# Half-size products for two more token blocks, paired masks, and V rows copied on the chip in a windowed attention plus squared-relu layer on one core

## The chip, the cores and the metric

The kernel runs on one core of a Trainium2 chip. The metric is device microseconds (us) of one execution; three runs of the kernel before took 288.63, 288.63 and 288.92 us, median 288.63. A profiled execution of the same kernel gives the trace that all readings below come from. Five engines work beside each other: TensorE (PE in the profile, with its weight loads as PEld), VectorE (DVE), ScalarE (ACT), GpSimd (POOL) and SyncE (SP). Here POOL does nearly nothing but issue loads, SP issues transposes and some loads and stores, and ACT issues stores beside its own work.

## The reference

Eight batches of 8 heads, 576 positions, 64 elements a head, all float32. Attention looks 32 positions to each side. Its output, 4608 tokens of 512 features, goes through a two-layer network whose hidden values (2048) are relu'd and squared.

```python
scores = q @ k.T / sqrt(64)                  # per batch and head
scores = where(abs(pos_q - pos_k) <= 32, scores, -1e9)
attn   = softmax(scores)
x      = (attn @ v) as [4608 tokens, 512]    # heads side by side
h      = x @ w_in                            # 512 -> 2048
out    = (relu(h) ** 2) @ w_out              # 2048 -> 512, float32
```

The kernel computes in bf16 with float32 sums in PSUM.

## The kernel before, in words

**Attention** goes in 24 steps (G in the code; three steps of 192 query positions for each batch, g = G % 3). The keys a step needs form two blocks of 128 positions (w = 0 and 1), starting at 192 g - 32 and 128 later. For each step:

- `load_qk` (L365) and `load_v` (L389) have POOL load q, k and v rows, casting to bf16 on the way. Step 0's k and step 2's q come as float32 through SP's and ACT's queues (`load_hw`, L374) and are cast on DVE and ACT. V goes into one of five tiles, `[128 positions, 2 key blocks, 8 heads, 66]`, a column of ones beside each head's 64. The second block of a step ends where the first block of the next step's first 64 rows do: block 1 of step g covers positions 192 g + 96 to 192 g + 224, and block 0 of step g + 1 begins at 192 g + 160. These 64 rows are loaded twice.
- q and k are turned by TensorE (`turn_pe`, L418, steps 0 to 8) or by a transposing DMA from SP (`turn_dma`, L449).
- `scores` (L468): 8 products for each key block (L495) into two PSUM banks, ACT takes the exponential into tile e (L518, 128x1024), DVE multiplies by a 0/1 mask into tile pt (L526, 128x1024). Each key block has a mask operation of its own.
- `pv` (L531): 8 products for each key block (L554) with V's ones giving the softmax sums, a reciprocal (L568), a scaled copy into xa or xb (L572), and a zeroing of half a PSUM region (L578 on ACT or L579 on DVE).
- `xturn` (L583) turns the result into `xt`, a ring of 1536 token columns.

**The first layer** takes tokens in blocks: 192, 192, 192, 192, 256, then 512 each (from token 1024). `mm1` (L637) is the standard form: for a 512-token block, 16 slices of hidden rows with 4 products of 512 columns each (L653), a relu for each slice out of PSUM (L629 on ACT or L628 on DVE) and a square for each two (L624 on DVE, L623 on ACT) into `gt`, a ring of 1024 tokens. `mm1s` (L696) is the half-size form, used for the blocks listed in `MM1S` (2560, 3072, 3584, 4096): 7 products of half-size matrices in place of 8. Four differences of x (L705) and, at the start of the kernel, sums of w_in (`sums_w1`, L684) are its operands; for each of 4 groups of hidden rows it runs 28 products of 256 columns (L733), a seed copy between two PSUM banks (L772), two copies out of PSUM (L634), two additions (L757), an in-place relu (L763 or L764), and relus and squares into `gt`.

**The second layer** is half-size for all but the first 512 tokens: `strassen` (L889) with products on L880, sums on L848, additions on L903, and stores. The first 512 tokens use `mm2` (L787, products on L798).

**What sets the order.** `record` (L929) lists all operations with their tiles; `rec` (L86) notes who reads and writes what. The string `ORDER` (L1039) gives each recorded operation, in that sequence, a letter for its engine (P TensorE, A ScalarE, D VectorE, G POOL, S SyncE) and a number; `apply` (L129) sorts by the number, and that sorted order is the order on every engine. Some operations can run on ACT or DVE (their `alt`), and the letter chooses. After the operations, ORDER gives each tile's slot in its pool (PSUM banks, e, pt, rt, oe, ...); a slot marked `w` is washed before use by one more product over zeros (L858). `fill` (L156) pads TensorE with small products over zeros (L295) until real work is dense. `emit` (L175) derives semaphore waits from the recorded reads and writes. No run-time choice is made: when an operation waits, everything behind it on its engine waits.

The dummy exponential of `setup_act` (L297), which makes ACT load its function table, has a place in ORDER like any other operation.

Of the kernel before, what the change touches and what calls it, by code (L numbers as in the profile page):

```python
# [4 lines left out]
ACTF = mybir.ActivationFunctionType  # L5
# [16 lines left out]
    MM1S=(2560, 3072, 3584, 4096),  # L22
# [9 lines left out]
    PAIR=(),  # L32
# [5 lines left out]
    SQP=1,  # L38
    FP=1,
    MP=0,  # L40
    S34=1,
    NZ=0,
    NV=5,
    NRAW=4,
    NE=2,
    NPT=3,
# [178 lines left out]
def dve(n, fast=True):  # L225
    return 153 + (0.52 if fast else 1.04) * n


class Gen:
# [130 lines left out]
    def source(self, t, b, g):  # L360
        t0, n = self.piece(t, b, g)
        src = (self.q if t == "q" else self.k)[b]
        return src[:, t0:t0 + n, :].rearrange("h (j p) d -> p j h d", j=2), n // 2

    def load_qk(self, t, b, g, key, after=None):  # L365
        s, h = self.source(t, b, g)
        G = 3 * b + g
        for j in range(2):
            dst = self.raw(t, b, g, j).rearrange("p (h d) -> p h d", h=8)
            self.p.rec("POOL", lambda e, j=j, dst=dst: e.dma_start(dst, s[:, j]),  # L370
                       writes=[self.rtag(t, b, g, j)], dma=(f"{t}{G % self.cfg['NRAW']}{j}", G), key=key, dur=500 + 3 * h,
                       move=(h // 2, 13.5), name=f"{t}{b}{g}{j}", after=after, slack=self.cfg["LSLACK"] if b > 1 else 0)

    def load_hw(self, t, g, eng, cast, u0, key):  # L374

        s, h = self.source(t, 0, g)
        for j in range(2):
# [4 lines left out]
            self.p.rec(eng, lambda e, j=j, f=f: e.dma_start(f.rearrange("p (h d) -> p h d", h=8), s[:, j]),  # L382
                       writes=[tag], dma=(f"h{t}{g}{j}", g), key=key, dur=450, move=(h // 2, 16), name=f"h{t}{g}{j}")
            fn = (lambda e, f=f, raw=raw: e.activation(raw, f, ACTF.Copy)) if cast == "ACT" else \
                (lambda e, f=f, raw=raw: e.tensor_copy(raw, f))
            self.p.rec(cast, fn, reads=[tag], writes=[self.rtag(t, 0, g, j)], key=self.cfg.get("CKEY", -100.0 - 14 + 100) + 3 * g,
                       dur=620 if cast == "ACT" else 600, name=f"c{t}{g}{j}")
# [13 lines left out]
    def load_w1(self, d, key):  # L401
        src = self.w_in[:, 512 * d:512 * d + 512].rearrange("(f p) c -> p f c", p=128)
        self.p.rec("POOL", lambda e: e.dma_start(self.W1[:, :, 512 * d:512 * d + 512], src),
                   writes=[("w1", d)], dma=(f"w1{d}", 0), key=key, dur=780, move=(32, 82), name=f"w1{d}")
# [13 lines left out]
    def turn_pe(self, t, b, g, key):  # L418
# [4 lines left out]
        v = Virt("bank", where=self.cfg.get("TB"))  # L423

        def f(e):
            ps = self.bank(v).bitcast(BF16)
            for j in range(4):
                for x in range(2):
                    mm = e.transpose(ps[:, n * j + h * x:n * j + h * x + h], raw[x][:, 128 * j:128 * j + 128],  # L429
                                     self.ID[0:h, 0:h])  # L430
            return mm
# [5 lines left out]
        def src():  # L437
            return self.bank(v).bitcast(BF16)[:, 0:4 * n].rearrange("p (j q) -> p j q", j=4)

        fa = lambda e: e.activation(dst, src(), ACTF.Copy)  # L440
        fd = lambda e: e.tensor_copy(dst, src())
        if t == "q":
            self.p.rec("ACT", fa, reads=[v], writes=w, key=key, dur=act(4 * n), name=f"ev{t}{b}{g}",
                       alt=("DVE", dve(4 * n), fd) if self.cfg["ALT"] else None, bias=0)
        else:
            self.p.rec("DVE", fd, reads=[v], writes=w, key=key, dur=dve(4 * n), name=f"ev{t}{b}{g}",
# [84 lines left out]
    def pv(self, G):  # L531
# [10 lines left out]
        for w in range(2):  # L542
# [15 lines left out]
            rd = [("v", G % NV, w), ("vset", G % NV), pt]  # L558
# [78 lines left out]
    def mm1(self, t0, n, ds, key, pair=False):  # L637
# [7 lines left out]
        v = Virt("bank", nb, clean=c >= 512, where=self.cfg.get("MB"))  # L645
        for h in range(nb):
# [10 lines left out]
            self.p.rec("PE", f, reads=[("xt", s) for s in steps] + [("w1", d // 4) for d in dh[:1]], writes=[(v, h)], uses=[v], key=key + 0.25 * h,  # L657
# [26 lines left out]
    def sums_w1(self, key):  # L684
        w, s, p = self.W1, self.SW, self.p
        for c in range(2):
            lo, hi = slice(512 * c, 512 * c + 512), slice(1024 + 512 * c, 1536 + 512 * c)
            a11, a12, a21, a22 = w[:, 0:2, lo], w[:, 2:4, lo], w[:, 0:2, hi], w[:, 2:4, hi]
            r1, r2 = [("w1", c)], [("w1", 2 + c)]
# [6 lines left out]
    def mm1s(self, t0, key):  # L696
# [11 lines left out]
        for m in range(4):  # L708
# [5 lines left out]
            wl, wh = [("w1", m // 2)], [("w1", 2 + m // 2)]  # L714
# [92 lines left out]
    def store(self, u, oe, dst, src, key, move):  # L807
# [3 lines left out]
                       move=move, name=f"st{u}", alt=("SP", 450, lambda e: e.dma_start(dst, src())), bias=self.cfg["STB"], after=self.stores[n - 8] if n >= 8 else None)  # L811
# [77 lines left out]
    def strassen(self, g, key):  # L889
# [5 lines left out]

        def out(i, j, rd, add, src, k, name):
            u = 4 * g + 2 * i + j
            oe = Virt("oe")
            o = lambda: self.oe(oe)
            if add is None:  # L900
# [139 lines left out]
D900 G1350 A1350 D1800 D8113 D8713 D9423 D10498 D8513 D10898 D12154 D7993 D7873 D9623 D10198 D7488 D7588 D21300 D10608  # L1040
D9908 D7198 D10298 D11118 D12354 D8313 D8933 D9223 D21953 D21015 D22183 D44470 D22063 D29378 S1350 D6598 S900 D4366
G1700 G2488 G4064 G5640 G4852 G3276 G7956 G7216 A900 A5559 A1780 A9625 G6428 G8696 G9580 G10464 G11348 G12128 G14572
G12908 G20264 G16140 G13688 G15352 G21044 G22564 P7268 A7873 P8259 A8811 P9715 A10350 D11468 P10140 A12274 D14614
P12224 D13658 D13928 A14839 P15537 D16007 D16277 P16505 P17033 A17473 P11390 D12554 P10907 A11459 P13176 A13811 D15299
# [132 lines left out]
```

## Time and profile before

| | |
|---|---|
| three runs, us | 288.63, 288.63, 288.92 |
| profiled execution, us | 288.32 |
| its span (first to last instruction), us | 286.5 |
| instructions | 7547 |
| bytes moved by DMA | 38.60 MB in 171106 packets |
| half-size first-layer products (L733) | 448 |
| standard first-layer products (L653) | 512, of them 192 with 512 columns |
| second-layer products (L880, L798) | 896 and 64 |

How to read the views: in a group's row stand line, engine, operation, the tile written and the tiles read, shape and count; then total busy us and mean ns of one; then how long the engine stood idle just before them, and what ended that wait. In a table of stretches each row is one stretch of time from the span's start, with busy us and counts for each engine, then the granted TensorE clock (1.00 is full), a DMA share and GB/s. The chain of work that ended last follows the execution backwards from its last instruction, each step to what released it. Matmul records of one group overlap each other in the trace, so counts and the pace of a back-to-back piece say more about TensorE than its busy share.

### The profile page before, as it was taken

To read this page: it belongs to the slowest core of one execution; us is meant where nothing else is said; L and a number is where in the kernel's file an instruction comes from. 1 tells how busy PE (TensorE), PEld (TensorE's weight loads), DVE (VectorE), ACT (ScalarE), POOL (GpSimd) and SP (SyncE) were. 2 spreads that over 40 slices of the span, in tenths; PEclk is the share of its full clock that TensorE was granted. 3 is DMA by queue.
4 is the path that set the end of the run, shared out by engine and by line. 5 is a ranking of instruction groups with operands and counts; after the bars stand their busy time and mean duration, and the time that the engine had idled before them with its cause. 6 is when DMAs were issued, how large, how long until landed. Compare 5 with 4: busy or idle time off the path is not lost.

```text
span 286.5 us, 7547 instructions
## 1 busy us (share of the span) xinstructions
PE 281.2 (98%) x3063; PEld 225.6 (79%) x3063; DVE 228.2 (80%) x427; ACT 200.3 (70%) x301; POOL 117.4 (41%) x153
## 2 busy tenths in 40 slices
PE   7999999999999999999999999999999999999995
PEld 7889857788657775667566888888988888888884
DVE  1878978868978798686998989988898978697731
ACT  2875738869783965777787978895688966778420
POOL 8999526999831927694332846000000000000000
PEclk9999999999999999999999999999999999999999
DMA  9999999999999999999999999995201221401033
GB/s 147 158 206 193 188 176 156 155 149 147 177 154 226 134 154 185 159 164 155 134 192 213 174 166 146 173 174 140 55 3 39 55 57 38 149 0 39 11 135 113
DMA packets 171106, 38.60 MB, mean 135 GB/s; under 512 B 158272, under 2 KB 170560, under 8 KB 171072
## 3 DMA queue, kind: packets, MB, share of 16 engines
q0 software_dynamic: 121920, 18.98, 99.4%
q1 hardware_dynamic: 42656, 13.51, 26.3%
q10 hardware_dynamic: 6496, 5.64, 7.2%
q8 instruction: 24, 0.39, 0.6%
q14 instruction: 10, 0.08, 0.2%
HBM read 38.80 MB, written 9.44 MB: 168 GB/s over the span
## 4 chain that ended last, share of the span: by engine, by line
PE 94%; DMA 2%; ACT 2%; DVE 1%; issue 0%; SPq 0%; DVEq 0%; ACTq 0%
PE ps L880 34%; PE ps L653 25%; PE ps L733 17%; PE ps L798 5%; PE ps L495 5%; PE ps L554 4%; DMA ts<-in_k_dram 2%; PE ps L429 2%; PE ps L295 1%; ACT kq L440 1%; PE ps L600 1%; PE ps L594 1%; DVE rt L757 0%; DVE rt L763 0%; ACT e L518 0%; DVE xa L572 0%
## 5 line engine op out<-in xcount | busy, mean ns | idle before, releaser
L653 PE MATMUL ps<-xt,w 128*128 128x192 bf16 (+2 forms) x512 | 77.4, 299 | 0.0
L629 ACT ACTIVATE rt<-ps 128x512 bf16<-128x512 f32 (+1 forms) x93 | 51.6, 566 | 30.1 <-PE ps L653 18.9
L653 PEld LDWEIGHTS ps<-xt,w 128*128 128x128 bf16 x512 | 44.6, 98 | 19.8
L396 POOL DMA_DIRECT2D v<-in_v_dram x48 | 41.9, 882 | 31.2 <-PE ps L554 31.2
L518 ACT ACTIVATE e<-ps 128x1024 bf16<-128x1024 f32 x48 | 48.1, 1021 | 8.3 <-PE ps L495 6.4
L880 PE MATMUL ps<-w,gt 128*128 128x256 bf16 x384 | 47.2, 273 | 0.0
L634 ACT ACTIVATE oe<-ps 128x512 f32<-128x512 f32 x56 | 32.6, 595 | 20.4 <-PE ps L880 10.9
L370 POOL DMA_DIRECT2D raw<-in_k_dram x46 | 36.8, 809 | 22.2 <-DMA kq<-raw 11.4
L623 ACT ACTIVATE gt<-rt 128x1024 bf16<-128x1024 bf16 (+2 forms) x49 | 41.6, 859 | 2.7 <-DVE rt L628 1.7
L880 PEld LDWEIGHTS ps<-w,gt 128*128 128x128 bf16 x384 | 36.7, 98 | 5.5
L526 DVE TENSOR_TENSOR pt<-e,mask 128x1024 bf16<-128x1024 bf16 x48 | 32.5, 685 | 8.5 <-ACT e L518 8.2
L370 POOL DMA_DIRECT2D raw<-in_q_dram x46 | 37.0, 812 | 5.2 <-DMA kq<-raw 2.9
L880 PE MATMUL ps<-ts,ss 128*128 128x256 bf16 x256 | 31.7, 273 | 0.0
L880 PE MATMUL ps<-ts,gt 128*128 128x256 bf16 x256 | 31.6, 273 | 0.0
L880 PEld LDWEIGHTS ps<-ts,ss 128*128 128x128 bf16 x256 | 24.7, 98 | 4.2
L880 PEld LDWEIGHTS ps<-ts,gt 128*128 128x128 bf16 x256 | 24.7, 98 | 3.5
L733 PE MATMUL ps<-xs,sw 128*128 128x256 bf16 x192 | 25.5, 273 | 0.0
L624 DVE TENSOR_TENSOR gt<-rt 128x1024 bf16<-128x1024 bf16 (+2 forms) x43 | 24.4, 576 | 1.3 <-ACT rt L629 1.1
L757 DVE TENSOR_TENSOR rt<-ps,oe 128x512 bf16<-128x512 f32 x32 | 21.6, 684 | 4.2 <-PE ps L733 3.8
L554 PEld LDWEIGHTS ps<-v,pt 128*128 128x128 bf16 x384 | 17.4, 98 | 3.9 <-DVE ps L579 0.8
L733 PEld LDWEIGHTS ps<-xs,sw 128*128 128x128 bf16 x192 | 18.5, 98 | 2.2
L554 PE MATMUL ps<-v,pt 128*128 128x65 bf16 x384 | 19.8, 194 | 0.1
(70 smaller groups left out, 370.2 us busy)
## 6 DMA issues: line engine op xcount, KB each, us to landing
out_dram<-oe ACTq DMA_DIRECT2D x20, 256.0 KB, 4.1
v<-in_v_dram POOLq DMA_DIRECT2D x32, 128.0 KB, 6.7
out_dram<-oe SPq DMA_DIRECT2D x16, 256.0 KB, 3.2
w<-in_moe_w_in_dram POOLq DMA_DIRECT2D x4, 512.0 KB, 9.6
w<-in_moe_w_out_dram POOLq DMA_DIRECT2D x4, 512.0 KB, 16.8
raw<-in_q_dram POOLq DMA_DIRECT2D x18, 96.0 KB, 6.2
raw<-in_q_dram POOLq DMA_DIRECT2D x14, 112.0 KB, 6.1
raw<-in_k_dram POOLq DMA_DIRECT2D x14, 112.0 KB, 6.5
```

Of the source, the lines that this page charges most:

```text
L370: self.p.rec("POOL", lambda e, j=j, dst=dst: e.dma_start(dst, s[:, j]), writes=[self.rtag(t, b, g, j)], dma=(f"{t}{G % self.cfg['NRAW']}{j ...
L396: self.p.rec("POOL", lambda e, j=j, lo=lo, hi=hi, k0=k0: e.dma_start(vt[lo - k0:hi - k0, j, :, 0:64], self.v[b, :, lo:hi, :].rearrange("h ...
L518: last = self.p.rec("ACT", lambda e, ef=ef, v=v: e.activation(ef(), self.bank(v, 0, 2), ACTF.Exp, scale=0.125), reads=[v], writes=tags, ke ...
L526: self.p.rec("DVE", lambda e, pf=pf, ef=ef, mb=mb, n=n: e.tensor_tensor(pf(y=0, n=n), ef(y=0, n=n).rearrange("p (w h q) -> p w h q", w=n, ...
L554: mm = e.matmul(ps[z:z + n, c:c + 65], ptt[:, 4 * (h % 2) + h // 2, z:z + n], vt[:, w, h, 0:65], start=((w == 0 or (z == 64 and split)) an ...
L623: alt = ("ACT", act(c), lambda e: e.activation(dst, src(), ACTF.Square)) if self.cfg["ALT"] else None
L624: self.p.rec("DVE", lambda e: e.tensor_tensor(dst, src(), src(), ALU.mult), reads=rd, writes=wr, key=key, dur=dve(c), name=name, alt=alt, ...
L629: return self.p.rec("ACT", lambda e: e.activation(dst(), src(), ACTF.Relu), reads=rd, writes=wr, key=key, dur=act(c), name=name, alt=alt, ...
L634: self.p.rec("ACT", lambda e: e.activation(dst(), src(), ACTF.Copy), reads=rd, writes=wr, key=key, dur=act(c), name=name, alt=alt, bias=se ...
L653: mm = e.matmul(ht[:, n * x:n * x + n], self.W1[:, ft, 128 * d:128 * d + 128], self.XT[:, ft, r:r + n], start=(ft == 0 and x == 0), stop=( ...
L733: mm = e.matmul(bk[:, 256 * x:256 * x + 256], lhs(k, 256 * m + 128 * x), rhs[:, k, :], start=start and x == 0 and k == 0, stop=(k == 1), s ...
L880: mm = e.matmul(op[:, 256 * y:256 * y + 256], lhs[:, l0[0] + k, a:a + 128], rhs[:, r0 + k, c0:c0 + 256], start=start and y == 0 and k == 0 ...
```

## The change

Three things are changed, and the whole order is written anew. The core of the diff:

```diff
 CFG = dict(
-    MM1S=(2560, 3072, 3584, 4096),
+    MM1S=(1536, 2048, 2560, 3072, 3584, 4096),
...
-    PAIR=(),
+    PAIR=(1024,),
...
-    MP=0,
+    MP=1,
...
+    VC=0,
...
-    NPT=3,
+    NPT=4,
...
+    def vcopy(self, G):
+        return G % 3 > 0 and G >= self.cfg["VC"]

     def load_v(self, b, g, key, after=None):
         G, NV = 3 * b + g, self.cfg["NV"]
         vt = self.V[G % NV]
         for j in range(2):
             k0 = 192 * g - 32 + 128 * j
             lo, hi = max(k0, 0), min(k0 + 128, S_)
+            if self.vcopy(G) and j == 0:
+                lo += 64
+                vs, vf = self.V[(G - 1) % NV][64:128, 1, :, 0:64], vt[0:64, 0, :, 0:64]
+                self.p.rec("DVE", lambda e, vs=vs, vf=vf: e.tensor_copy(vf, vs), reads=[("v", (G - 1) % NV, 1)], writes=[("vc", G % NV)],
+                           key=key + 2, dur=290, name=f"vc{b}{g}",
+                           alt=("ACT", act(512), lambda e, vs=vs, vf=vf: e.activation(vf, vs, ACTF.Copy)) if self.cfg["ALT"] else None,
+                           bias=self.cfg["ALTB"])
...
     def pv(self, G):
...
-            rd = [("v", G % NV, w), ("vset", G % NV), pt]
+            rd = [("v", G % NV, w), ("vset", G % NV), pt] + ([("vc", G % NV)] if w == 0 and cfg["VC"] < NG else [])
...
     def mm1(self, t0, n, ds, key, pair=False):
...
-            self.p.rec("PE", f, reads=[("xt", s) for s in steps] + [("w1", d // 4) for d in dh[:1]], writes=[(v, h)], uses=[v], key=key + 0.25 * h,
+            got = self.p.rec("PE", f, after=got, reads=[("xt", s) for s in steps] + [("w1", d // 4, d % 4 // 2 if d // 4 in self.cfg["W1H"] else 0) for d in dh[:1]], writes=[(v, h)], uses=[v], key=key + 0.25 * h,
                        dur=4 * len(dh) * (n / 2.4 + 2.5), name=f"A{t0}.{dh[0]}")
...
 ORDER = """
-D900 G1350 A1350 D1800 D8113 D8713 D9423 D10498 D8513 D10898 D12154 D7993 D7873 D9623 D10198 D7488 D7588 D21300 D10608
+D900 G1350 A48064 D5616 D7398 D7888 D8308 D9513 D8108 D9623 D11270 D4966 D5086 D1385 D9413 D2000 D9843 D10680 D5326
...
```

- **Half-size products:** the blocks at tokens 1536 and 2048 go from `mm1` to `mm1s`. The block at 1024 stays standard, with `PAIR`: two slices of hidden rows share two PSUM banks, one relu of 1024 and one square of 1024.
- **Masks:** with `MP=1`, steps 6 to 23 (those whose two key blocks are recorded together) take both slots of e and two neighbouring slots of pt, and one DVE operation of 128x2048 masks both key blocks after the second exponential. Steps 0 to 5 keep one mask operation for each block. The pool pt has 4 slots, not 3.
- **V rows:** in steps with g = 1 or 2 the first 64 rows of key block 0 are copied from the step before's tile (partitions 64 to 127 of block 1 to partitions 0 to 63 of block 0), on DVE or ACT, and the load takes the other rows only. PV of block 0 waits for the copy as well.
- **Order:** 1480 operations in place of 1418: on TensorE 466 in place of 442, DVE 447 for 427, ACT 339 for 322 (with stores that it issues), POOL 149 for 149, SP 79 for 78. Three slots are marked for a wash, where one was. In ORDER's first line the third entry is the dummy exponential: it stands at A1350 before and at A48064 after, behind ACT's casts of step 2's q.
- **Unused:** the diff also adds options (a split w_in load, another packing of q and k rows, a split last store) whose settings leave them off.

More of the change, by code (lines that the diff above doesn't have):

```diff
@@ L38 @@
     SQP=1,
+    W1H=(),
+    TAIL=0,
     FP=1,
-    MP=0,
+    MP=1,
     S34=1,
     NZ=0,
+    VC=0,
+    PR=0,
     NV=5,
@@ L894, in strassen @@
         u2, p5 = Virt("oe"), Virt("oe")
+        last = self.cfg["TAIL"] and g == NTOK // 512 - 1
         def out(i, j, rd, add, src, k, name):
@@ L899, in out @@
             o = lambda: self.oe(oe)
+            if last and add is None and i:
+                for y in range(2):
+                    c = slice(256 * y, 256 * y + 256)
+                    self.copy(lambda c=c: o()[:, c], lambda c=c: src()[:, c], rd, [(oe, y)], k, name + "ab"[y], 256, uses=[v, oe])
+                    dst = self.out[512 * g + 256 * i + 128 * y:512 * g + 256 * i + 128 * y + 128, 256 * j:256 * j + 256]
+                    self.store(f"{u}{'ab'[y]}", (oe, y), dst, lambda c=c: o()[:, c], k, (8, 21), uses=[oe])
+                return
             if add is None:
```

269 lines of the change are left out of this document (149 added, 120 removed), and 9 rows, old and new, of the table ORDER.

## The prediction

> **What bounds the kernel now.** I read the page's totals first, then the chain that ended last, then tables by stage, because an average over this kernel mixes attention, first layer and second layer.
>
> ```profile
> span 286.5 us, 7547 instructions
> ...
> PE 281.2 (98%) x3063; PEld 225.6 (79%) x3063; DVE 228.2 (80%) x427; ACT 200.3 (70%) x301; POOL 117.4 (41%) x153
> ...
> DMA  9999999999999999999999999995201221401033
> ...
> PE 94%; DMA 2%; ACT 2%; DVE 1%; issue 0%; SPq 0%; DVEq 0%; ACTq 0%
> ```
>
> TensorE carries 94% of the chain and looks busy for 98%. Ends of matmuls are modelled, so I check that figure with paces, from pieces of the chain in which products run back to back:
>
> ```profile
> 151.69 3.45 PE ps L653 x16
> 155.14 0.51 PE ps L554 x16
> ...
> 174.68 0.69 DVE rt L757
> ...
> 177.22 0.70 DVE rt L757
> ...
> 190.23 0.55 PE ps L495 x16
> ...
> 246.50 9.17 PE ps L733 x84
> ```
>
> A product of 512 columns (L653, first layer as it stands) takes 3.45/16 = 0.2156 us, one of 256 columns (L733, half-size) 9.17/84 = 0.1092, a PV product 0.51/16 = 0.0319, a score product 0.55/16 = 0.0344. Now the stage that the change rewrites, 100 to 170 us, counted by line on TensorE, without the weight loads:
>
> ```profile
> L653 PE MATMUL ps<-xt,w 128*128 128x512 bf16 x132 | 31.3, 379 | 0.0
> L880 PE MATMUL ps<-w,gt 128*128 128x256 bf16 x112 | 13.9, 273 | 0.0
> L880 PE MATMUL ps<-ts,gt 128*128 128x256 bf16 x86 | 10.7, 273 | 0.0
> L880 PE MATMUL ps<-ts,ss 128*128 128x256 bf16 x64 | 8.0, 273 | 0.0
> L554 PE MATMUL ps<-v,pt 128*128 128x65 bf16 x136 | 6.9, 194 | 0.0
> L495 PE MATMUL ps<-kq 64*128 64x128 bf16 x144 | 5.6, 217 | 0.0
> L733 PE MATMUL ps<-xt,w 128*128 128x256 bf16 x22 | 2.9, 272 | 0.0
> L733 PE MATMUL ps<-xs,sw 128*128 128x256 bf16 x4 | 0.6, 272 | 0.0
> ```
>
> 132 x 0.2156 + (262 + 26) x 0.1092 + 136 x 0.0319 + 144 x 0.0344 = 28.46 + 31.45 + 4.34 + 4.95 = 69.2 us of 70. TensorE is the bound there, with at most 0.8 us of slack. What stands close behind it shows in the stretches:
>
> ```profile
> 100.00:170.00 70.00, 70.00 (x700) 48.75 (x698) 59.14 (x103) 51.47 (x70) 35.89 (x46) 1.00 1.87 165
> 170.00:232.00 62.00, 61.91 (x662) 54.30 (x660) 55.00 (x101) 49.26 (x82) 6.61 (x9) 1.00 0.83 105
> 160.00:170.00 10.00, 10.00 (x111) 8.48 (x109) 9.64 (x18) 7.96 (x12) 4.95 (x7) 1.00 2.48 156
> 170.00:180.00 10.00, 9.91 (x107) 8.61 (x106) 8.91 (x16) 8.55 (x16) 6.61 (x9) 1.00 2.22 181
> 250.00:260.00 10.00, 10.00 (x94) 8.95 (x93) 9.75 (x17) 8.44 (x15) 0.00 (x0) 1.00 0.03 9
> 234.00:264.00 30.00, 30.00 (x277) 26.89 (x275) 24.17 (x43) 21.33 (x35) 0.00 (x0) 1.00 0.17 56
> ```
>
> Columns after the stretch's length: PE, weight loads, VectorE (DVE), ScalarE (ACT), POOL, each busy us with its count, then the granted clock (1.00 throughout). From 100 to 232 us DVE and ACT together work 114.14 + 100.73 = 214.87 of 264 us, 81%. The fullest ten microseconds, 250 to 260, reach 18.19 of 20 (91%) with TensorE still full.
>
> The Trainium skill, "Perfetto Trace Analysis", section Identifying the Most-Contended Engine, says that matmul busy time is no good measure and names weight-load busy share instead. By that, 48.75 of 70 would leave TensorE 30% of room and the change's saving on it would be worth nothing. The counted stream above disagrees; I keep the rule as part of the rival of no change.
>
> **The change part by part.** Durations of ACT (first four) and DVE operations between 100 and 232 us:
>
> ```profile
> L518 ACT ACTIVATE e<-ps 128x1024 bf16<-128x1024 f32 x26 | 26.0, 1022 | 5.3 <-PE ps L495 4.4 <-ACT oe L634 0.5 <-DVE pt L526 0.3
> L629 ACT ACTIVATE rt<-ps 128x512 bf16<-128x512 f32 x42 | 24.7, 596 | 12.5 <-PE ps L653 7.9 <-PE ps L733 4.1
> ...
> L623 ACT ACTIVATE gt<-rt 128x512 bf16<-128x512 bf16 x11 | 6.8, 630 | 0.1
> L772 ACT ACTIVATE ps<-ps 128x512 f32<-128x512 f32 x11 | 6.3, 586 | 1.2 <-PE ps L733 1.0
> ...
> L526 DVE TENSOR_TENSOR pt<-e,mask 128x1024 bf16<-128x1024 bf16 x26 | 17.7, 683 | 4.5 <-ACT e L518 4.3
> L757 DVE TENSOR_TENSOR rt<-ps,oe 128x512 bf16<-128x512 f32 x20 | 13.4, 684 | 1.6 <-PE ps L733 1.3 <-ACT oe L634 0.2
> ...
> L624 DVE TENSOR_TENSOR gt<-rt 128x1024 bf16<-128x1024 bf16 x12 | 8.2, 685 | 0.7 <-ACT rt L629 0.6
> ...
> L848 DVE TENSOR_TENSOR gt<-gt 128x2048 bf16<-128x2048 bf16 x5 | 6.1, 1213 | 0.0
> ...
> L624 DVE TENSOR_TENSOR gt<-rt 128x512 bf16<-128x512 bf16 x7 | 2.8, 419 | 0.0
> ...
> L763 DVE TENSOR_SCALAR rt<-rt 128x1024 bf16<-128x1024 bf16 x6 | 2.7, 470 | 0.1
> ```
>
> *Products.* The token blocks at 1536 and 2048 (512 tokens each) now run 64 products of 512 columns: 64 x 0.2156 = 13.80 us. Half-size they are 112 of 256 columns: 112 x 0.1092 = 12.23. TensorE saves 1.57 a block, 3.14 in all. The new order marks three slots to be washed (a 512-column product over zeros, 0.2156) in place of one: +0.43. TensorE net: **-2.71 us**.
>
> *What the two blocks cost DVE and ACT.* Today a block needs 16 relus and 8 squares of 1024: 16 x 0.596 + 8 x 0.685 = 15.0. Half-size it needs 4 differences of x (TENSOR_TENSOR of 128x512, as L624's: 0.419) and, for each of 4 groups, a seed copy 0.586, two relus and two copies out of PSUM (four at 0.596), two additions 0.684, one in-place relu 0.470, one square of 1024 at 0.685 and two of 512 at 0.419: 6.33. Sum 1.68 + 25.32 = 27.0. Two blocks add **+23.96 us** on the two engines.
>
> *Masks.* Steps 6 to 23 get one mask operation of 2048 instead of two of 1024: by L848's row 1.213 for 2 x 0.683, -0.153 each. 26 masks lie in this stretch, so 13 pairs: -1.99. The merged operation waits on DVE for both exponentials (1.022 apart), and whatever DVE has queued behind it waits too; against that it waits once, not twice. Ends: 13 x 1.02 = +13.3 of DVE stall, and -4.3 (all that L526 now waits for ACT). The order puts other work ahead of the mask as it does today; I take 0, nearest to the measured 4.5 us in 26.
>
> *V rows.* Sixteen steps load 64 rows less and copy 64x512 on the chip. No row shows this copy: between half of L763's (0.235) and ACT's L623 (0.630) I take 0.419 as L624's has the same width. About 9 lie in the stretch: 2.1 to 5.7, taken **+3.77**. It waits for a load of the step before, which must be there anyway for that step's PV. What the smaller load brings I take as nothing:
>
> ```profile
> POOL v L396 <- PE ps L554: 31.2, 5, 10.4
> ```
>
> V's loads stand 31.2 us waiting for a buffer that PV still reads, and no compute engine's wait names a V load. Each remaining load is issued at the same place in POOL's queue, with nothing moved past it. If that cover were gone, the two ends are +0.63 (one copy on the path at the start) and a gain of a few tenths there.
>
> *The rest.* Block 1024 merges its relus in pairs (16 x 0.596 - 8 x 1.022 = -1.36 on ACT), but 132 of the 192 L653 products of 512 columns come after 100 us, so that block lies before the stretch, and it holds two banks longer: 0. The ordering edge inside a pair is on TensorE's own queue: 0. Each half-size block stages its results in the same six slots of oe that the stores use: 0 as long as stores land in time, inside the loss below if not. At the start, the dummy exponential that brings ACT's table early is put far back in the order, so the load falls to the first cast:
>
> ```profile
> 1.20 1.28 ACT L299 ACT_TABLE_LOAD   x1 [1.20 <-PEq L1162]
> ...
> 4.93 0.63 ACT L384 ACTIVATE raw<-ts 96x512 bf16<-96x512 f32 x1 [2.23 <-DMA ts<-in_q_dram]
> 7.79 1.66 ACT L440 ACTIVATE kq<-ps 128x896 bf16<-128x896 bf16 x2 [2.23 <-PE ps L429]
> ```
>
> If the load stands behind that cast's data wait, 4.93 + 1.28 + two casts of 0.63 = 7.47, before the 7.79 at which ACT is next needed. Hidden: 0, with 0.3 us of cover; at worst +1.0.
>
> *The sum.* In the stretch DVE and ACT would have 214.87 + 23.96 - 1.99 + 3.77 = 240.6 us of work, while TensorE needs 132 - 2.71 = 129.3 us. That is 93% of both engines, fuller than any ten microseconds now. If both hold 91%, the stretch takes 240.6 / 1.82 = 132.2 us: the gain is gone (-0.2). Every microsecond of such work that the order moves out of the stretch gives back 1/1.82 = 0.55; all 2.71 come back with 5.3 us moved. Later there is room: 234 to 264 holds 45.5 of 60, 9.1 under 91%. Earlier there is little, since the DMA digit is 9 in every slice up to 190 us and loads set how far attention can run ahead. Between nothing and 5.3 I take a third, 1.8, as most of that work feeds products inside the stretch. Gain: 1.8 x 0.55 - 0.2 = **0.8 us**.
>
> The profiled execution took 288.32 us, 1.8 over its span; 288.32 - 0.8 = 287.5. The median of the three runs is 288.63, 0.31 above it, so the forecast is **287.8**.
>
> **The rivals.** *All of it comes through:* the engines run at 93% and TensorE keeps its 2.71: 285.9. For it: engine idle time now is mostly waiting for TensorE; against: nothing that full has been seen. 0.12. *No change:* 91% holds and nothing moves, -0.2, so 288.8; or TensorE has hidden room, as the page quoted above would have it. 0.20. *The engines become the bound:* in 160 to 180 us, where a half-size block meets attention, they do 35.06 of 40, 88%, and exactly there the chain leaves TensorE for DVE (L757 at 174.68 to 177.92). If 88% is the ceiling beside attention, 235.3 us of work (5.3 moved out) take 235.3 / 1.754 = 134.2, so +2.2: 290.8; it decides against the change as soon as the engines can't hold 240.6/264 = 91% and nothing moves. 0.20. *Paired masks hold up PV:* PV of the first half waits 1.022 + 0.53 longer, of the second 0.53; uncovered, 13 pairs at 0.53 make 6.9 us, of which I price the two fifths that could fall where TensorE has nothing else, 2.7 over the forecast: 290.5. Against it: PV waits for no mask today. 0.05.
>
> The Trainium skill, "Perfetto Trace Analysis", section Optimizing Scalar/DVE Operations, says grouping helps where the engine is saturated and splitting where it only causes bubbles elsewhere. At 86% (114.14 of 132) DVE lies between; by the second half the masks would cost as in the last rival, by the first they save the 2 us counted above.
>
> **How the numbers follow.** The forecast (part of the gain, 286.2 to 288.0) has 0.43. A measurement of this kernel tells about 0.2%, 0.58 us, from no change. Faster: 0.43 + 0.12 = 0.55; same 0.20; slower 0.20 + 0.05 = 0.25. The range leaves out most of the full gain and half of the engine-bound cases: 286.1 to 290.5.
>
> **What would show it.** Half-size products (L733's line) 672 in number and L653's 512-column ones 64; between 100 and 230 us DVE and ACT above 90% together. If the forecast is right, new gaps in TensorE's stream there sum to about 1.9 us. If ACT and DVE stay under 88% while TensorE idles, the third rival holds; if ACT's first copy of L440 starts later than 7.79 us by more than the spread of the run, the table load is not hidden. I am wrong if the paces change, or if attention itself is late.

## The result, and the profile after

Ten runs of the changed kernel had a median of 289.69 us (288.37 to 293.15); ten runs of the kernel before on the same chip 288.60 (288.39 to 288.92). The ratio is 1.0033, 95% interval 1.0018 to 1.0048: slower by a third of a per cent, where the forecast was 287.8 and faster. The profiled execution took 288.98 us. Medians and ranges here and below are over all runs of a kernel; ratios and their intervals leave out runs more than 1.5% above the fastest run of the same kernel.

Line numbers from here on are those of the kernel after: L770 (half-size products) was L733, L742 (differences of x) L705, L690 (standard products) L653, L917 (second layer) L880, L562 (mask) L526, L590 (PV) L554, L531 (scores) L495; L491, L649 and L652 are SP's transposes of q and k, of xa and of xb.

The page's rows that answer to those shown of before, then rows of the table of stretches:

```profile
span 287.1 us, 7749 instructions
...
PE 277.9 (97%) x3136; PEld 235.2 (82%) x3151; DVE 241.5 (84%) x447; ACT 212.5 (74%) x319; POOL 114.8 (40%) x153
...
PE 87%; DMA 4%; DVE 3%; POOL 3%; ACT 1%; issue 1%; SPq 1%; DVEq 0%; POOLq 0%
```

```profile
100.00:232.00 132.00, 128.99 (x1433) 112.23 (x1434) 118.77 (x208) 107.16 (x165) 45.40 (x59) 1.00 1.27 138
```

```profile
60.00:100.00 40.00, 39.27 (x428) 27.85 (x434) 35.43 (x61) 31.99 (x39) 22.28 (x29) 1.00 1.81 148
100.00:112.00 12.00, 9.55 (x116) 7.65 (x115) 8.51 (x16) 7.96 (x10) 10.68 (x14) 1.00 1.80 199
```

The two shorter stretches of before:

```profile
60.00:100.00 40.00, 40.00 (x441) 28.87 (x439) 32.55 (x59) 30.59 (x45) 27.33 (x36) 1.00 1.98 166
100.00:112.00 12.00, 12.00 (x127) 8.45 (x125) 10.74 (x18) 8.55 (x11) 4.99 (x7) 1.00 1.73 165
```

Three things are to be seen. TensorE's share of the chain fell from 94 to 87%, and DMA, DVE and POOL took what it lost. DVE and ACT together work 225.9 of 264 us from 100 to 232 (86%), not the 240.6 of the forecast. And TensorE loses 2.4 of 12 us in one place, 100 to 112, **where both engines are emptier than before**, and full engines would not look like that. The timelines of TensorE and then of DVE show the place; the bracket is the idle time before a row and what ended it:

```profile
106.64 0.42 PE L590 MATMUL ps<-v,pt 128*128 128x65 bf16 x8
108.83 0.61 PE L770 MATMUL ps<-xt,w 128*128 128x256 bf16 x4 [1.77 <-DVE xs L742]
...
111.79 1.03 PE L917 MATMUL ps<-w,gt 128*128 128x256 bf16 x8 [0.63 <-DVE rs L604]
```

```profile
103.49 0.68 DVE L885 TENSOR_TENSOR ss<-gt 128x1024 bf16<-128x1024 bf16 x1
107.10 0.43 DVE L742 TENSOR_TENSOR xs<-xt 128x512 bf16<-128x512 bf16 x1 [2.93 <-DMA xt<-xb]
107.56 0.89 DVE L742 TENSOR_TENSOR xs<-xt,xs 128x512 bf16<-128x512 bf16 x2
108.36 0.42 DVE L742 TENSOR_TENSOR xs<-xt 128x512 bf16<-128x512 bf16 x1
```

L770 at 108.83 is the first product of the half-size block at token 1536. Its four differences of x (L742) head DVE's queue from 104 us on, wait 2.93 us for a transposing DMA that brings the block's last tokens, and then take 1.7 us. Everything behind them on DVE waits too: the reciprocal that frees the next PSUM region ends TensorE's second wait. The chain of work that ended last goes through the same place, and SP's issues say why the tokens are late:

```profile
100.26 1.65 SPq L649
101.95 4.96 DMA xt<-xb
107.10 0.44 DVE xs L742
```

```profile
91.57 1.22 SPq L491 DMA_TRANSPOSE kq<-raw  x1
92.85 0.57 SPq L848 DMA_DIRECT2D out_dram<-oe  x1
93.47 1.19 SPq L649 DMA_TRANSPOSE xt<-xa  x1
94.76 2.77 SPq L491 DMA_TRANSPOSE kq<-raw  x2
97.58 2.63 SPq L652 DMA_TRANSPOSE xt<-xb  x1
100.26 1.65 SPq L649 DMA_TRANSPOSE xt<-xa  x1
101.95 1.27 SPq L652 DMA_TRANSPOSE xt<-xb  x1
```

From 91.57 on SP issues without a pause, 1.2 to 2.6 us each, and the last of them is the one that the differences wait for. Below, an operation of SP is called by its step: td301 turns the second part of q and k for batch 3, step g = 0; T9b turns tokens of step 9 out of xb. The issue at 101.95 is T9b. What holds the whole row back is its first entry, td401 at 91.57: it waits for the load of k401, which landed at 91.52. That load was late on POOL, and POOL had waited for td301. SP's row for td310 and td301, the two issues' time to landing, and POOL's row:

```profile
67.24 3.70 SPq L491 DMA_TRANSPOSE kq<-raw  x2
```

```profile
kq<-raw SPq DMA_TRANSPOSE x2, 8.3
```

```profile
78.85 0.77 POOL L377 DMA_DIRECT2D raw<-in_k_dram  x1 [6.67 <-DMA kq<-raw]
```

td301 is the second of the two: issued at 68.56, landed at 78.29. So the **theory**: td301 is queued behind td310, which serves a later step and waits for a later load; td301 lands late; POOL stands 6.67 us for the buffer that td301 reads; k401 is late; td401 blocks SP; the tokens of block 1536 land at 106.91, just when TensorE arrives; and the half-size form, unlike the standard one, puts four DVE operations between tokens and first product. That td301 was slow to land is not only its place in line: the one issued ahead of it, td310, took 6.9 us from issue to landing, and td301 9.7. In the kernel before the same tokens landed later still, at 108.27, and the standard block began right behind them, in TensorE's row at 108.41 without a wait (no run puts the standard form into the new order, so this part of the theory is read from two traces and not tested):

```profile
108.10 0.42 PE L554 MATMUL ps<-v,pt 128*128 128x65 bf16 x8
108.41 2.97 PE L653 MATMUL ps<-xt,w 128*128 128x512 bf16 x13
```

The **rival** is the forecast's own step: DVE and ACT have too much to do.

### The profile page after: what moved, and what is told of

Its sections match the earlier page's. It is cut to its first block, busy times and chain, and to the rows that moved or that the text cites. A ratio compares the mean times of both kernels' runs of the same rounds, so it can differ in the third digit from the quotient of the medians.

```text
span 287.1 us, 7749 instructions
## 1 busy us (share of the span) xinstructions
PE 277.9 (97%) x3136; PEld 235.2 (82%) x3151; DVE 241.5 (84%) x447; ACT 212.5 (74%) x319; POOL 114.8 (40%) x153
## 4 chain that ended last, share of the span: by engine, by line
PE 87%; DMA 4%; DVE 3%; POOL 3%; ACT 1%; issue 1%; SPq 1%; DVEq 0%; POOLq 0%
PE ps L917 32%; PE ps L770 25%; PE ps L690 13%; PE ps L835 5%; PE ps L590 4%; PE ps L531 4%; POOL raw L377 2%; DMA raw<-in_k_dram 2%; DMA xt<-xb 2%; PE ps L463 2%; DVE pt L562 1%; PE ps L636 1%; PE ps L299 1%; PE ps L630 1%; SPq L649 1%
## 5 line engine op out<-in xcount | busy, mean ns | idle before, releaser
L665 ACT ACTIVATE rt<-ps 128x512 bf16<-128x512 f32 (+2 forms) x75 | 44.9, 610 | 17.4 <-PE ps L690 7.9
L670 ACT ACTIVATE oe<-ps 128x512 f32<-128x512 f32 x69 | 40.8, 594 | 21.7 <-PE ps L917 14.5
L554 ACT ACTIVATE e<-ps 128x1024 bf16<-128x1024 f32 x48 | 48.7, 1021 | 6.6 <-PE ps L531 4.4
L917 PE MATMUL ps<-w,gt 128*128 128x256 bf16 x384 | 47.8, 273 | 0.7 <-DVE rs L604 0.6
L690 PE MATMUL ps<-xt,w 128*128 128x192 bf16 (+2 forms) x379 | 46.6, 271 | 0.3
L659 ACT ACTIVATE gt<-rt 128x512 bf16<-128x512 bf16 (+2 forms) x59 | 45.3, 785 | 1.5 <-DVE oe L949 0.8
L917 PEld LDWEIGHTS ps<-w,gt 128*128 128x128 bf16 x384 | 36.7, 98 | 5.9 <-ACT e L554 0.9
L690 PEld LDWEIGHTS ps<-xt,w 128*128 128x128 bf16 x384 | 32.7, 98 | 8.6 <-DVE xt L646 0.3
L770 PE MATMUL ps<-xs,sw 128*128 128x256 bf16 x288 | 39.3, 273 | 0.0
L794 DVE TENSOR_TENSOR rt<-ps,oe 128x512 bf16<-128x512 f32 x48 | 32.8, 686 | 3.9 <-PE ps L770 3.1
L562 DVE TENSOR_TENSOR pt<-e,mask 128x2048 bf16<-128x2048 bf16 (+1 forms) x30 | 30.2, 1006 | 2.8 <-ACT e L554 2.5
L917 PE MATMUL ps<-ts,gt 128*128 128x256 bf16 x256 | 31.9, 273 | 0.0
L917 PE MATMUL ps<-ts,ss 128*128 128x256 bf16 x256 | 31.9, 273 | 0.0
L770 PEld LDWEIGHTS ps<-xs,sw 128*128 128x128 bf16 x288 | 27.8, 98 | 3.3
L770 PE MATMUL ps<-xt,w 128*128 128x256 bf16 x192 | 27.4, 273 | 2.3 <-DVE xs L742 1.8
L917 PEld LDWEIGHTS ps<-ts,ss 128*128 128x128 bf16 x256 | 24.5, 98 | 3.3
L917 PEld LDWEIGHTS ps<-ts,gt 128*128 128x128 bf16 x256 | 24.5, 98 | 3.1
L770 PEld LDWEIGHTS ps<-xt,w 128*128 128x128 bf16 x192 | 18.2, 98 | 4.9 <-DVE xs L742 1.9
```

The costliest lines, as they stand in the source:

```text
L554: last = self.p.rec("ACT", lambda e, ef=ef, v=v: e.activation(ef(), self.bank(v, 0, 2), ACTF.Exp, scale=0.125), reads=[v], writes=tags, ke ...
L562: self.p.rec("DVE", lambda e, pf=pf, ef=ef, mb=mb, n=n: e.tensor_tensor(pf(y=0, n=n), ef(y=0, n=n).rearrange("p (w h q) -> p w h q", w=n, ...
L659: alt = ("ACT", act(c), lambda e: e.activation(dst, src(), ACTF.Square)) if self.cfg["ALT"] else None
L665: return self.p.rec("ACT", lambda e: e.activation(dst(), src(), ACTF.Relu), reads=rd, writes=wr, key=key, dur=act(c), name=name, alt=alt, ...
L670: self.p.rec("ACT", lambda e: e.activation(dst(), src(), ACTF.Copy), reads=rd, writes=wr, key=key, dur=act(c), name=name, alt=alt, bias=se ...
L690: mm = e.matmul(ht[:, n * x:n * x + n], self.W1[:, ft, 128 * d:128 * d + 128], self.XT[:, ft, r:r + n], start=(ft == 0 and x == 0), stop=( ...
```

## The experiments

Each time stands beside runs of the kernel before on the same chip (medians 288.55 to 288.77). In the diffs of ORDER the operation is written ahead of its entry.

**1. Token transposes ahead (t9_early).** Only SP's order changes:

```diff
-td410 S91380  td400 S92670  T10b S94788  T10a S96038  T9b S97288
+td400 S91380  T9b S93100  T10a S94788  T10b S96038  td410 S97288
```

> All work is that of the kernel after; only SP's order changes: of the five transposes issued between 94.8 and 103.2 us, the three that turn tokens 1728 to 2111 go ahead of a k/q transpose (td410) that is needed later. Tokens-late theory (the half-size block at 1536 starts before its tokens have landed, and VectorE's in-order queue stands on its x differences): the last token transpose is issued about 2.5 us sooner, VectorE's 2.93 us of idle time ahead of the first difference shrinks below 0.7, TensorE's 3.1 us of gaps between 106.9 and 111.8 shrink below 1, and the time falls by 2 to 3 us against the kernel after, to 286.5 to 287.5, under the kernel before. Load theory (VectorE and ScalarE are too full from 100 to 232 us, the forecast's step): their work is the same, so the time stays within 0.5 us of the kernel after, at 289 to 290, and a gap that closes at 107 opens again later.

Median 286.60 us (285.85 to 287.76), ratio 0.9925 (0.9904 to 0.9945). No operation was removed, and the slowdown of 0.3% became a gain of 0.75%. In its profile, the fastest of the six runs, T9b was issued at 93.31 in place of 101.95 and landed at 97.89. Not all of these 8.6 us come from the edit: td401, which stands ahead of the changed entries, already went out at 86.09 in place of 91.57 in this execution. The load theory, at 289 to 290, does not hold as the cause of the loss.

**2. The head of the chain alone (td301_first).**

```diff
-td301 S67828  td310 S66538
+td301 S66540  td310 S67830
```

> The kernel after with the exchange of td301 and td310 on SP alone; the token transposes keep their places, T9b last. Chain read from the traces: td301 waits on SP behind td310, which waits for q310's load; td301 lands at 78.29; POOL's queue has stood 6.67 us for the buffer that td301 reads, so the load k401 lands at 91.52; td401, at the head of SP's queue, is issued at 91.57 and all token transposes behind it are late. In t9_early's profile td301 had landed at 75.92 and td401 was issued at 86.09. If this chain is right, the exchange alone is enough: td401 issued at 88 to 89, the last token transpose landed by 104, no stall at 107, median 286.5 to 287.2. If only the order of the token transposes matters: the stall at 107 stays, 288.8 to 289.7.

Median 286.65 (286.25 to 290.17, ten of twelve runs under 287.3), ratio 0.9941 (0.9917 to 0.9965). SP, POOL, DVE and TensorE in its timelines:

```profile
67.43 1.23 SPq L491 DMA_TRANSPOSE kq<-raw  x1
```

```profile
88.42 2.27 SPq L491 DMA_TRANSPOSE kq<-raw  x1
...
98.00 2.11 SPq L652 DMA_TRANSPOSE xt<-xb  x1
```

```profile
74.36 0.77 POOL L377 DMA_DIRECT2D raw<-in_k_dram  x1 [2.25 <-DMA kq<-raw]
```

```profile
104.67 0.42 DVE L742 TENSOR_TENSOR xs<-xt 128x512 bf16<-128x512 bf16 x1
```

```profile
107.22 0.42 PE L590 MATMUL ps<-v,pt 128*128 128x65 bf16 x8
107.48 0.60 PE L770 MATMUL ps<-xt,w 128*128 128x256 bf16 x4
```

td301 is issued at 67.43, 1.13 us sooner, and lands at 73.79, 4.50 sooner. POOL goes on at 74.36, td401 is issued at 88.42, T9b, still last, at 98.00; it lands at 103.12, the differences start without a wait, and so does the first product. The page's chain is TensorE's again:

```profile
PE 92%; POOL 3%; DMA 2%; ACT 1%; issue 1%; DVE 0%; POOLq 0%; ACTq 0%
```

A step 40 us ahead of the stall decides it. DVE and ACT are *busier* here than in the kernel after (229.2 against 225.9 of 264 us), and TensorE loses less:

```profile
100.00:232.00 132.00, 131.36 (x1457) 113.94 (x1457) 120.58 (x211) 108.59 (x169) 45.17 (x59) 1.00 1.23 134
```

**3. Both exchanges (both_early).**

> As t9_early (the three token transposes moved ahead on SP), and a second exchange on SP: td301, which turns step 9's second half of k and q, goes ahead of td310, which is for step 10 and waits for a later load. In the kernel after, step 9's score products waited for td301 (landed 78.29, wait 0.42 us; in the profiles of loose and light it landed at 80.86 and 80.30 and the wait was 2.2 us). Late-data theory: td301 is issued 1.3 to 1.7 us sooner, that wait is gone in every run, the runs lie within 1 us of each other, and the median falls 0.2 to 0.8 us under t9_early's 286.6, to 285.8 to 286.4. If the wait at 78 us was only a sign of a disturbed run: the same median as t9_early and the same spread of 1.9 us.

Median 286.56 (286.12 to 287.20), ratio 0.9935 (0.9923 to 0.9946): no gain over either alone, as if the two were two ways out of the same delay; the expected 0.2 to 0.8 us under t9_early did not come. Only its spread is smaller, in five runs; that the wait at 78 us costs t9_early anything isn't shown. Against the kernel before it is 2.06 us faster, and it is the base of some later runs.

**4. TensorE's own wait loosened (loose).**

```diff
-                    rd = st[0] + st[1] + wl + wh + [("xs", x) for x in range(4)] + [("sw", x, m // 2) for x in range(4)]
+                    rd = st[0] + wl + [("sw", x, m // 2) for x in range(4)] if t0 in (1536, 2048) else st[0] + st[1] + wl + wh + [("xs", x) for x in range(4)] + [("sw", x, m // 2) for x in range(4)]
```

> Work and order of the kernel after; the first product of each group of the half-size blocks at 1536 and 2048 no longer waits for all four x differences, but only for the 256 tokens that it reads. Tokens-late theory, if the wait of TensorE's own first product is what costs: the first product starts at 106.9 in place of 108.8, the gaps there fall from 3.1 to about 1 to 2 us (the third product still needs a difference, and VectorE still stands 2.9 us with reciprocals and zeroings behind it), and the time falls by 1 to 2 us against the kernel after. If VectorE's standing queue is what costs, not that one wait: a gain under 0.7 us, with the gaps moved to products that follow. Load theory: no change beyond 0.3 us.

Median 290.04, but the runs go from 286.18 to 293.50, and the ratio, 0.9984 (0.9948 to 1.0019), settles nothing: both expectations are missed. Its profile is of a run of 291.37, and is read only for where the wait went:

```profile
109.59 0.43 DVE L742 TENSOR_TENSOR xs<-xt 128x512 bf16<-128x512 bf16 x1 [2.84 <-DMA xt<-xb]
```

```profile
109.80 0.60 PE L770 MATMUL ps<-xt,w 128*128 128x256 bf16 x4
111.97 0.62 PE L531 MATMUL ps<-kq 64*128 64x128 bf16 x16 [1.57 <-ACT ps L809]
```

The tokens themselves landed only at 109.40 in this run, 2.5 us later than in the profile of the kernel after. The first product no longer waits, and the next operation does. How much of the loss is TensorE's own wait and how much DVE's standing queue stays open.

**5. Less engine work, same tokens (light).** The 24 squares of the half-size blocks at 1536 and 2048 run on 16 of 256 columns, and the rest of `gt` keeps old values there:

```diff
-                self.square(lambda: self.rt(z).rearrange("p (d t) -> p d t", d=2), dst, [z], tag(ds, 0), kk, "g" + nm, 512)
+                c = 16 if t0 in (1536, 2048) else 256
+                self.square(lambda: self.rt(z).rearrange("p (d t) -> p d t", d=2)[:, :, 0:c], dst[:, :, 0:c], [z], tag(ds, 0), kk, "g" + nm, 512)
...
```

> Work and order of the kernel after, but the 24 squares of the half-size blocks at 1536 and 2048 work on 16 of 256 columns, so the second layer reads old values in the rest for these tokens. That takes some 16.3 us of square time (12.1 ScalarE, 4.1 VectorE) down to about 5, so 11 us of engine work less between 110 and 170 us, and nothing of the tokens' arrival. Load theory: 11 us less work at two engines that hold 91 per cent between them would give back all that the forecast lost to load, 1.9 us or more; 287 to 287.5. Tokens-late theory: the stall at 107 to 112 us stays, the time is within 0.6 us of the kernel after, 289 to 290.

Median 288.95 (287.14 to 291.84), ratio 1.0020 (0.9994 to 1.0046): not told apart from the kernel after. The stretch from 100 to 232 us holds 118.02 + 100.36 = 218.4 us of DVE and ACT work, 7.5 less than after and 10.8 less than td301_first:

```profile
100.00:232.00 132.00, 131.24 (x1450) 113.32 (x1450) 118.02 (x211) 100.36 (x168) 45.12 (x59) 1.00 1.27 138
```

TensorE's busy time in the stretch is 131.24 us here and 131.36 in td301_first, neither of which has the stall at 107: up to 229 us, engine work costs it nothing that shows. By the forecast's own rule both lie under the 235.3 us at which load begins to count, so this run says nothing on the price above that. The expectation of the tokens-late theory, that the stall at 107 stays, is missed in this profile: TensorE is busy 11.73 of 12 us from 100 to 112. Its long wait is for td301's data, at 80 us, 2.0 us:

```profile
PE ps L531 <- DMA kq<-raw: 2.0, 1, 2.0
```

There td301 landed at 80.30. The same late transpose cost TensorE its time sooner, and TensorE then reached the tokens after they had landed (106.56).

**6. More engine work, tokens in time (t9_full, both_full).** 38 DVE and 28 ACT operations on scratch tiles, spread over 100 to 232 us:

```diff
+            p.rec("DVE", lambda e: e.tensor_tensor(s1[:], zz[:], zz[:], ALU.mult), reads=["id"], writes=[("sc", 1)], dur=200, name=f"ex{n}")
...
+            p.rec("ACT", lambda e: e.activation(s2[:], zz[:], ACTF.Square), reads=["id"], writes=[("sc", 2)], dur=280, name=f"ey{n}")
```

> t9_early with 38 multiplications of 128x128 on VectorE and 28 squares of 128x128 on ScalarE added on scratch tiles that nothing reads, spread evenly from 100 to 232 us: some 7.6 + 7.8 = 15.4 us of engine work more, so that the two engines reach about 241 of 264 us, the 91 per cent that the forecast had reckoned with. If that fullness costs time as the forecast said, 1 to 2 us slower than t9_early (287.6 to 288.6). If engine work of this size is absorbed, within 0.5 us of t9_early; then the forecast's load step is wrong in kind, not only in size.

> both_early with the 66 scratch operations of t9_full (15.4 us of engine work between 100 and 232 us). t9_full's median was 1.95 us above t9_early's, but its five quietest runs lay at 287.2 to 287.5, 0.8 above. On an order whose runs scatter less: 0.7 to 1.0 us above both_early if the quiet runs tell the cost of the work, 1.5 to 2.5 us if the median did; within 0.3 us if engine work is absorbed.

t9_full: median 288.55 (287.21 to 292.52), ratio 0.9991 (0.9967 to 1.0015), 1.95 us above t9_early: taken by itself this is what the load theory expected. Five of its twelve runs lie at 287.2 to 287.5, the others from 288.2 up. both_full: 287.34 (286.74 to 289.37, and one run of 1084.01 that no trace explains), ratio 0.9966 (0.9950 to 0.9982), 0.78 us above both_early. The stretch's rows, both_early and then both_full:

```profile
100.00:232.00 132.00, 131.35 (x1462) 114.00 (x1462) 120.52 (x211) 108.88 (x169) 45.09 (x59) 1.00 1.25 135
```

```profile
100.00:232.00 132.00, 130.94 (x1443) 112.67 (x1444) 124.89 (x247) 113.78 (x195) 45.30 (x59) 1.00 1.29 138
```

The small operations overlap in the records, so the engines' busy time grew by 9.3 us, not by 15.4: from 229.4 to 238.7 of 264 (90%). The profile of both_full is of a run of 289.37 us, 2.0 above the median; what it lost beyond both_early's profile shows as a wait of 2.1 us for a q and k transpose at 87.7, ahead of the stretch. t9_full's profile, of a run of 287.46, has the same picture in the stretch: 237.9 us of engine work for 230.0 in t9_early. In both pairs TensorE's busy time there falls from 131.35 to 130.94, by 0.41 us.

So engine work near 90% is not free: 0.41 us in the traces, 0.78 in the medians on one order, 1.95 on the other. The forecast's rule charges 0.55 only above 235.3 us (91% beside TensorE's 129.3), and so 1.9 us for both_full and 1.4 for t9_full. On both_early's order that is more than twice too much; on t9_early's it is not refuted, because no trace shows what the slower runs of t9_full waited for.

**7. V rows loaded twice again (no_vcopy, t9_novc, both_novc).** Copies left out in the kernel after, in t9_early and in both_early:

```diff
-    VC=0,
+    VC=99,
```

> Work and order of the kernel after, but V rows are loaded twice as before: no copies on the chip, 16 loads of 128 rows for 16 loads of 64 rows and 16 copies. Theory that the copies cost (0.29 us on VectorE each, 11 of them, and 0.63 on ScalarE, 5 of them): a gain of 0.2 to 0.6 us. Theory that the smaller loads help (8192 fewer packets on POOL's queue, which shares the DMA engines with the transposes): the last transpose of the tokens lands later than 106.91 us, by some tenths up to 1 us, and the time grows by 0.3 to 1 us. My expectation: within 0.4 us of the kernel after.

> t9_early with V rows loaded twice again: no copies, 8192 packets more. With the tokens' stall out of the way this shows what the V edit does by itself. If copies cost as in the forecast (3.8 us of engine work in 100 to 232 us, 0.55 us of time for each us not absorbed): up to 0.5 us faster than t9_early. If nothing waits for V either way: within 0.3 us of it. If the smaller loads help the transposes to land: 0.3 to 1 us slower, with waits of TensorE at 78 or 107 us.

> both_early with V rows loaded twice. In t9_novc (288.54 in median, t9_early 286.6) the loads k401 and V came later and TensorE waited 1.06 us for a V load. If the packets cost through POOL's queue and the transposes behind it, and the exchange of td301 takes most of that chain away: 286.8 to 287.8, a little slower than both_early. If the 8192 packets cost whatever the order: 288 or more. If t9_novc's loss was the spread of that run: within 0.3 us of both_early.

Medians 289.49, 288.54 and 287.24; ratios 0.9999 (0.9968 to 1.0030), 1.0000 (0.9974 to 1.0026) and 0.9960 (0.9935 to 0.9985). On the kernel after the copies make no difference that shows; on t9_early they are worth 1.9 us; on both_early 0.7, with intervals that overlap. In t9_novc's profile TensorE waited for a V load (the 1.06 us of the last expectation is more than this wait; TensorE's idle time from 100 to 112 us is 1.05 in all):

```profile
PE ps L590 <- DMA v<-in_v_dram: 0.9, 1, 0.9
```

So on t9_early's order the copies help, and this wait is a part of it that the trace shows. How they help is not settled. td401 went out at 92.15 in t9_novc and at 86.09 in t9_early, but at 90.35 and 90.11 in t9_full and t9_split, which have the copies and the same order on SP: one profile of each can't tell the packets from the scatter. The Trainium skill, "DMA: Bandwidth & Descriptors", section Issuing engines are not separate DMA queues, says that loads started by different engines share the same 16 DMA engines and interleave. No run here shows what that sharing costs, or parts it from the longer queue on POOL.

**8. Masks apart again (t9_split, both_split2).** One operation for each key block; in t9_split the first mask stands 1.04 us after its exponential's place in the order, in both_split2 both stand where the merged one stood:

```diff
-    MP=1,
+    MP=0,
```

> t9_early with a mask operation for each key block again, as in the kernel before (18 more operations, 0.153 us of VectorE more for each pair). Forecast's step (masks worth 2.0 us of engine work in 100 to 232 us, and hold-up taken as 0): 0 to 0.5 us slower than t9_early if engine work counts, the same within 0.3 us if it does not. Rival that paired masks hold up PV: faster by 0.5 us or more.

> both_early with two mask operations at the place of the one (the first directly ahead of the second), in steps 6 to 23. In t9_split the first masks stood earlier in VectorE's queue, so its 3.7 us mix the number of operations with their places. If the number counts (0.15 us of VectorE for each pair, 2.8 us in all, on a full engine): 0.2 to 0.7 us slower than both_early. If the places were what cost in t9_split: within 0.3 us of both_early. If separate masks as such cost 3 us: 289 or more.

t9_split: 290.35 (289.23 to 293.68), ratio 1.0058 (1.0041 to 1.0075), 3.8 us above t9_early. both_split2: 286.73 (286.50 to 287.59), ratio 0.9944 (0.9925 to 0.9963), 0.17 above both_early, which the intervals don't tell apart. The number of operations hardly counts; their place does. In t9_split TensorE is busy 128.94 us from 100 to 232, 2.4 less than in t9_early, in many small gaps. One of them, in DVE's row and in TensorE's behind it:

```profile
195.30 0.69 DVE L562 TENSOR_TENSOR pt<-e,mask 128x1024 bf16<-128x1024 bf16 x1 [0.72 <-ACT e L554]
```

```profile
198.15 0.43 PE L590 MATMUL ps<-v,pt 128*128 128x65 bf16 x8 [0.32 <-DVE ps L615]
```

A mask that comes to the head of DVE's queue before its exponential is done stops all behind it, here a zeroing that PV waits for. That the other gaps have the same cause is argued from this one.

## Why the prediction was wrong

**The products: right, as far as the runs part them.** The profile after counts 672 half-size products on the line of the former L733. With the tokens in time the kernel is 2.06 us faster than before (both_early) of the 2.71 forecast; t9_early's median is 2.17 below, 286.60, where the rival "all of it comes through" said 285.9. Neither of the other two edits makes this gain alone: without the V copies (both_novc) 1.3 us are left, with the masks apart (both_split2) 1.8. No run has the half-size blocks without the new order, so what that order gives by itself stays open. The page of the Trainium skill quoted in the prediction, "Perfetto Trace Analysis", names the share of peak arithmetic beside the weight loads in the section Identifying the Most-Contended Engine; the prediction took the weight loads alone. With them at 70% of the stretch the saving would have been worth nothing, and the 2.06 us, with the counted 69.2 of 70 us, speak against that use of it.

**The step that failed: "In the stretch DVE and ACT would have ... 240.6 us of work ... If both hold 91%, the stretch takes ... 132.2 us: the gain is gone".** The term that was mis-sized is the work that moves out of the stretch, taken as 1.8 us. The added work as such was foreseen well (+25.7 reckoned; the busy rows of the two pages give 241.5 + 212.5 - 228.2 - 200.3 = +25.5 over the whole span), but of it only 11.1 us came into 100 to 232 in the kernel after, and 14.5 in both_early. So 11 to 15 us lay elsewhere, well over the 5.3 that, by the forecast's own rule, bring all of the gain back. "Earlier there is little" was the error: in both_early 7.2 us more than in before lie ahead of 100 us, and 3.2 behind 232. With 225.9 us the kernel after is under the 235.3 at which the rule begins to charge, and yet it lost, and two edits that leave all engine work as it is win 3 us back (experiments 1 and 2): load is not the cause. The price above 235.3 was too high on both_early's order and is open on t9_early's (experiment 6).

**What stood in its place was not priced at all.** The four differences were counted as work, 1.68 us a block. That they are also a wait, with the last transpose of 512 tokens in front and the first product behind, is not in the sum. The prediction's last sentence says "I am wrong ... if attention itself is late", without a rival or a price for it. SP's and DVE's order around 100 us in the new string ORDER could have been read beforehand. The late transposes cost about 3.0 us in the medians (289.69 less 286.65; the gaps in the one profile after sum to 2.4), and the forecast's 0.8 of gain became 1.1 of loss. How much of that is the half-size form and how much the order of SP alone is not shown: loose, which was to part them, settles nothing.

**Luck.** The sum took off 1.9 us for load, which did not cost the kernel after its time, and nothing for the late transposes, which cost 3.0. These two errors cancel in part, and without that the miss of 1.9 us would be larger. That 289.69 lies between 286.1 and 290.5 is luck too: the upper part of that range stood for full engines.

**The test that I set was a bad one.** "If ACT and DVE stay under 88% while TensorE idles, the third rival holds": they stayed at 86% and TensorE idled, and the rival was false (experiments 1 and 2: the same work, 3 us less). Engines that wait for the same late data are emptier too. Low busy time beside an idle TensorE says only that something else is late; what it is must be read from what ended the waits.

**Paired masks: right** on the hold-up: 18 operations of 1.22 us, as reckoned from 1.213, which waited 0.3 us for ACT in all. A gain from them doesn't show (0.17 us in experiment 8). **V rows: half right.** The copies took 0.33 us on DVE and 0.62 on ACT in the mean, inside the bounds; to take "what the smaller load brings" as nothing was wrong on t9_early's order, as experiment 7 shows. **The table load: right.** It was hidden, and more easily than reckoned: it ran from 1.90 to 3.18 us and did not stand behind the cast's wait for data, and ACT's first copy began at 7.83 for 7.79 before.

Of the 2.71 us, 0.65 are missing in both_early. TensorE waits for a k load in the first 20 us (0.6 us in the profile after, 0.8 in both_early's, 1.4 in td301_first's, none in before's list of waits); that this is the rest is argued, not shown.

## What to carry to other kernels

When a stage gets a new form, look first at what must be there before its first product, which queue brings it, and what waits in line on the engine that prepares it: here the form saves 2.7 us of products by the forecast's count, its differences stood 2.9 us waiting for their data, and two numbers in SP's order decided the sign. Follow a late arrival back through its queues until an entry is found that waits for something not needed yet; in a static order that entry may stand 40 us ahead of the stall. Total load says little as long as the work can move: find out how much of it falls in the stretch before pricing it.

## What the runs showed of the hardware

A transposing DMA is slow to give and slow to land: SP spent 1.2 to 2.6 us in issuing each, and in the kernel after the nine that turn q and k between 66 and 104 us took a median of 6.1 us from issue to landing, td301 9.7. Of the pair td310 and td301, the one issued second took longer in both orders: 6.9 and 9.7 us in the kernel after, 6.4 and 8.6 in td301_first with td301 ahead. So an issue 1.13 us sooner landed 4.50 us sooner.

Two exchanged entries moved the median by 3.0 us. The scatter differs too: the kernel after ran from 288.37 to 293.15, the kernel before beside it within 0.6 us, both_early within 1.1 in five runs. Whether the order makes that scatter is not shown: td301_first has a run of 290.17, and the kernel before spread over 1.5 us in the rounds of the experiments, apart from three runs further out.
